# Scores of a chunked linear attention: the second sequence of a pair held with its halves exchanged

## The chip, the cores and the metric

The kernel runs on one NeuronCore of one Trainium2 chip. TensorE multiplies matrices (its records are split into weight loads, PEld, and matmuls, PE), VectorE (DVE) and ScalarE (ACT) do elementwise work and empty PSUM, GpSimd (POOL) issues indirect transfers, and SyncE (SP) issues most others. The metric is the device time of one execution in microseconds.

## The reference

Two blocks follow each other. The first is a gated linear attention: for each of 4 sequences and 8 heads, a 48 by 48 state decays by a gate per key dimension and takes in one outer product per token.

```python
f = 1.0 / (1.0 + np.exp(-f_logit))
for t in range(S):                                   # S = 768, D = 48
    state = f[:, :, t, :, None] * state + np.einsum('bhd,bhe->bhde', k[:, :, t], v[:, :, t])
    y[:, :, t] = np.einsum('bhd,bhde->bhe', q[:, :, t], state)
```

The heads of a token are then joined to a row of 384, and the 3072 rows go through a mixture of experts with two levels of gates: a softmax over 4 groups picks a group, a softmax over the 4 experts of that group picks an expert, and the row's output is the product of both weights times `relu(x @ w1[g, e]) @ w2[g, e]`, with a hidden size of 1024.

## The kernel before

**The attention stage.** A sequence is cut in 6 chunks of 128 tokens. A unit is one chunk of a pair of sequences, so there are 12 units, `i = 0` to `11`; even ones belong to the first pair (`s = 0`), odd ones to the second. Inside a chunk, the recurrence is written as matrix products. With the running sum `cs` of the negative log gates (a matmul with the triangle `tri`, L600), queries are scaled by `exp(-cs)` (`eq`) and keys by `exp(cs)` (`kh`). Then the stages of a unit are:

- `load`, L568 to L575: f, q, k and v arrive on SP's queue with tokens on the partitions, one transfer for each tensor of a unit (two for the first f).
- `c` bounded, `g` gated (exp, ln, `cs`, exp; the last row of `eq` goes to `ends` by a small transfer on POOL's queue), `m` multiplied (VectorE scales q and k).
- `t` turned: 16 transposes put the head dimension on the partitions, two heads to a tile (48 rows at 0 and at 64); ACT copies them to `Tq` and `Tk`.
- `b` decayed, for every second unit: `ends` is turned, and the chunk's decay goes to `decays`.
- `s` scored, L648 to L664: for each of the two sequences, 16 products of 64 keys with all 128 queries fill two PSUM banks (one for each head of a tile); then VectorE multiplies each bank with `tri`, which gives zero where the key is later than the query, and writes `am`.
- `n` stated: products `kh` by `v` give the chunk's own state (`ds`), and VectorE adds and decays it.
- `w` weighed: products of the old state with the queries (L699, not in the first chunk), then of `v` with `am` (L704), into the same banks; ACT copies them to `xT`.
- `d` done: `xT` times the turned gate weights `gw` gives the routing logits, transposed (`lT`); ACT copies them, and a matmul with `fold` turns them and adds the two heads' halves (`lg`, L724); VectorE copies them out.
- `x` listed: 8 transposes bring the rows back to tokens on partitions (`x_ps`), and they are stored.

A product in 32-bit floats leaves two matmul records in the trace, a transpose one: 32 score products are the x64 of a unit.

**Order.** On TensorE, VectorE, ScalarE and SP the order is written out by hand. Lists of steps (`BEGIN` for units 0 to 2, then `EVEN`, `ODD` and a few lists for the last units) call one stage's next part at a time; `s s s s` stands for scores and masks of one sequence, then of the other. `p` writes constants and pads, `h` turns the gate weights (`turn_gates`, L109), and `r` takes the routing of a finished chunk on by one part. In the steady part TensorE's order is x_ps, tr (turns), cs of the next unit, ap (scores), y of L699, lT of the unit before, y of L704, ds, lg. All tiles in PSUM are of one bank and come from one pool of eight. [...]

**The rest.** After unit 11 two early experts, chosen from the first four chunks, run while the routing of the last chunk is finished (until about 168 us); then the 16 experts run one after the other over gathered rows until the end. At the end of the program stands a branch that is not taken with these inputs: `scan` computes the attention in another way when the gates decay too fast.

```python
        EVEN = "l+2 d-2 n-1 r r r x-1 x-1 t t t t g+1 g+1 x-1 r s s s s c+2 w d-1 g+2 w g+2 n m+1 m+1".split()
        ODD = "l+2 d-2 b n-1 r r x-1 x-1 t t t t g+1 g+1 x-1 r s s s s c+2 w d-1 g+2 w g+2 n m+1 m+1 r n".split()
```

## Time and profile before

| | |
|---|---|
| median of 3 runs | 429.12 us (428.27 to 431.68) |
| the profiled execution | 421.97 us, its span 420.2 us |
| PE busy | 408.4 us, 97% of the span |
| DVE busy | 267.1 us, 64% |
| ACT busy | 156.7 us, 37% |
| scores (L660), PE | 768 records, 23.8 us |
| masks (L663), DVE | 48 operations, 29.8 us, mean 682 ns |
| products with v (L704), PE | 384 records, 23.4 us |

The profile is of one execution. A group line gives the source line, the engine, the operation, what is written and read (out<-in), the shape and the count, then busy time and mean duration. In a timeline each line begins with start and length in microseconds from the start of the span; instructions of one kind that follow each other are merged. The chain of work that ended last is followed back from the end to what released each step. A line of waits reads: engine and instruction, then what it waited for, the total in us, how often, and the longest.

### The profile page before, as it was taken

What the parts mean: (1) busy time and instruction counts of PE and PEld (TensorE: products, weight loads), DVE (VectorE), ACT (ScalarE), POOL (GpSimd) and SP (SyncE); (2) the same over time, 40 slices, a digit from 0 to 9 for tenths busy, and PEclk for the clock granted to TensorE, in tenths of its full rate; (3) what the DMA queues carried; (4) which work ended last, traced back from release to release, by engine and by line L of the source; (5) the groups of instructions that cost most, each with busy time, mean ns of one, the idle gap of its engine ahead of it and who ended that gap; (6) DMA issues with size and microseconds to landing.
All of it is one profiled execution on the core that took longest, in us unless ns stands there. A gap on an engine that the chain in (4) does not pass through costs nothing.

```text
span 420.2 us, 10089 instructions
## 1 busy us (share of the span) xinstructions
PE 408.4 (97%) x4067; PEld 383.3 (91%) x4067; DVE 267.1 (64%) x778; ACT 156.7 (37%) x341; POOL 83.2 (20%) x127
## 2 busy tenths in 40 slices
PE   4999999999999999999999999999999999999995
PEld 2888999999889887979999999999999999999992
DVE  6665686868798760650599785495685685595240
ACT  5667666666774421211122121221231231231220
POOL 4000010101012027201021331312222221110230
PEclk9999999999999999999999999999999999999999
DMA  9999999998899819978448385595585785585010
GB/s 168 177 179 178 183 179 179 165 154 146 168 331 404 316 29 365 365 286 308 156 176 288 109 327 189 207 321 162 233 302 146 285 289 192 233 318 159 29 46 25
DMA packets 132121, 88.98 MB, mean 212 GB/s; under 512 B 102630, under 2 KB 122700, under 8 KB 132066
## 3 DMA queue, kind: packets, MB, share of 16 engines
q1 hardware_dynamic: 125666, 75.50, 66.2%
q0 software_dynamic: 5792, 11.92, 9.5%
q8 instruction: 34, 0.56, 0.6%
q10 hardware_dynamic: 608, 0.83, 0.6%
q14 instruction: 21, 0.17, 0.1%
HBM read 78.71 MB, written 9.83 MB: 211 GB/s over the span
## 4 chain that ended last, share of the span: by engine, by line
PE 53%; issue 29%; DMA 8%; POOL 6%; ACT 1%; POOLq 1%; DVE 1%; SPq 0%
PE hp L441 12%; PE yo L477 6%; DMA out_dram<-yt,xg 6%; PE ap L660 5%; PE y L704 5%; PE cs L600 4%; PE yo L462 4%; POOL out_dram L452 4%; PE x_ps L744 3%; PE lT L719 3%; PE tr_q L634 3%; POOL xg L395 2%; PE tr_k L634 2%; PE y L699 2%; PE ds L677 2%
## 5 line engine op out<-in xcount | busy, mean ns | idle before, releaser
L441 PE MATMUL hp<-xe,w 128*128 128x128 f32 (+14 forms) x864 | 138.6, 320 | 0.0
L441 PEld LDWEIGHTS hp<-xe,w 128*128 128x128 f32 x864 | 135.8, 190 | 0.8
L477 PE MATMUL yo<-h,w 128*128 128x230 f32 (+13 forms) x672 | 115.8, 333 | 0.0
L424 DVE STREAM_TRANSPOSE yr<-yT 32x192 f32<-32x192 f32 (+1 forms) x208 | 70.5, 339 | 70.4 <-ACT yT L478 67.8
L477 PEld LDWEIGHTS yo<-h,w 128*128 128x128 f32 x672 | 113.7, 190 | 0.2
L417 DVE STREAM_TRANSPOSE xe<-xg 32x192 f32<-32x192 f32 (+1 forms) x208 | 69.7, 335 | 8.6 <-PE hp L441 5.6
L442 ACT ACTIVATE h<-hp 128x256 f32<-128x256 f32 (+14 forms) x72 | 34.4, 478 | 103.6 <-PE hp L441 103.6
L452 POOL DMA_INDIRECT out_dram<-yt,xg x32 | 34.4, 1076 | 150.4 <-ACT yt L449 144.8
L478 ACT COPY yT<-yo 128x230 f32<-128x230 f32 (+13 forms) x42 | 13.5, 326 | 80.5 <-PE yo L477 80.5
L663 DVE TENSOR_TENSOR am<-ap,tri 128x512 f32<-128x512 f32 x48 | 29.8, 682 | 17.8 <-PE ap L660 17.8
L395 POOL DMA_INDIRECT xg<-x_dram,rows_p x30 | 29.6, 987 | 51.5 <-DMA out_dram<-yt,xg 27.4
L600 PE MATMUL cs<-ld_f,tri 128*128 128x384 f32 x48 | 19.4, 529 | 5.6 <-DVE eq L538 5.5
L660 PE MATMUL ap<-Tq,Tk 48*64 48x128 f32 x768 | 23.8, 272 | 0.3 <-ACT Tk L635 0.3
L704 PE MATMUL y<-am,v 128*64 128x128 f32 x384 | 23.4, 273 | 0.0
L660 PEld LDWEIGHTS ap<-Tq,Tk 48*64 48x64 f32 x768 | 20.8, 133 | 2.1 <-issue 1.1
L704 PEld LDWEIGHTS y<-am,v 128*64 128x64 f32 x384 | 21.4, 137 | 0.6 <-DVE am L663 0.5
L462 PE MATMUL yo<-w,h 128*128 128x384 f32 x64 | 21.3, 486 | 0.0
L462 PEld LDWEIGHTS yo<-w,h 128*128 128x128 f32 x64 | 11.9, 190 | 7.4
L600 PEld LDWEIGHTS cs<-ld_f,tri 128*128 128x128 f32 x48 | 8.6, 200 | 9.7 <-issue 6.0
L607 POOL DMA_DIRECT2D ends<-eq x10 | 5.4, 541 | 60.2 <-ACT eq L601 60.2
L449 ACT ACTIVATE yt<-yr,xg 128x384 f32<-128x384 f32 (+13 forms) x26 | 14.4, 604 | 5.4 <-DVE yr L424 5.4
L707 ACT COPY xT<-y 128x512 f32<-128x512 f32 x24 | 12.9, 589 | 9.3 <-PE y L704 9.3
(170 smaller groups left out, 386.0 us busy)
## 6 DMA issues: line engine op xcount, KB each, us to landing
w<-in_moe_w_dram SPq DMA_DIRECT2D x34, 1536.0 KB, 10.3
qh<-in_q_dram SPq DMA_DIRECT2D x12, 384.0 KB, 6.6
ld_k<-in_k_dram SPq DMA_DIRECT2D x12, 384.0 KB, 6.4
v<-in_v_dram SPq DMA_DIRECT2D x12, 384.0 KB, 7.2
ld_f<-in_f_logit_dram SPq DMA_DIRECT2D x11, 384.0 KB, 6.4
x_dram<-x_kept SPq DMA_DIRECT2D x2, 1536.0 KB, 11.6
x_dram<-x POOLq DMA_DIRECT2D x2, 384.0 KB, 7.2
x_dram<-x ACTq DMA_DIRECT2D x2, 384.0 KB, 7.7
```

Of the source, the lines that this page charges most:

```text
L395: nc.gpsimd.indirect_dma_start(out=w["x"][:, j, :], out_offset=None, in_=x_dram[0:1 + top, :], in_offset=bass.IndirectOffsetOnAxis(ap=rows ...
L417: squares(w, lambda n, k_, rk, g, rg: nc.vector.transpose(out=xT[rg, 0:n, k_], in_=x[rk, 0:n, g]))
L424: squares(w, lambda n, k_, rk, g, rg: nc.vector.transpose(out=y[rk, 0:n, g], in_=yT[rg, 0:n, k_]))
L441: nc.tensor.matmul(hp[:, o, :], lhsT=w1[:, ko, (f + o) * P:(f + o + 1) * P], rhs=w["xT"][:, ko, :], start=(ko == 0), stop=(ko == KO - 1))
L442: nc.scalar.activation(h[:, f:f + 2, :], hp, AF.Relu)
L452: sent = nc.gpsimd.indirect_dma_start(out=out, out_offset=bass.IndirectOffsetOnAxis(ap=w["x"][0:m, j, DM + 1:RW].bitcast(U32), axis=0), in ...
L462: nc.tensor.matmul(yp, lhsT=w["h"][:, fo, :], rhs=w2[:, fo, :], start=(fo == 0), stop=(fo == FO - 1))
L477: nc.tensor.matmul(yp, lhsT=w2[:, fo, m * P:(m + 1) * P], rhs=w["h"][:, fo, :], start=(fo == 0), stop=(fo == FO - 1))
L600: nc.tensor.matmul(cs.rearrange("t h d -> t (h d)"), lhsT=tri, rhs=nl[:, b], start=True, stop=True)
L660: nc.tensor.matmul(ap[r][half, a, :], lhsT=w["Tk"][rows, b, a, half], rhs=w["Tq"][rows, b, a, :], start=True, stop=True)
L663: nc.vector.tensor_tensor(am[:, r], ap[r], tri.unsqueeze(1).broadcast_to((P, HP, P)), OP.mult)
L704: nc.tensor.matmul(ys[r][DP * b:DP * b + DP, a, :], lhsT=w["v"][:, b, 2 * a + r, :], rhs=w["am"][b][:, r, a, :], start=(c == 0 and a == 0) ...
```

## The change

In the second sequence of each pair, the partitions 0 to 63 now hold the later 64 tokens of a chunk, and 64 to 127 the earlier ones. It is loaded that way, so every load of a unit becomes three transfers: the first sequence, and the two halves of the second. The running sum of the second sequence uses an exchanged triangle `tri_s`, its chunk end stands on partition 63 in place of 127, and token numbers are corrected by 64 in either half.

In the scores, the later 64 keys of a chunk are multiplied only with the later 64 queries; the part that would be multiplied by zero is left unwritten in PSUM, and the `am` tiles, now kept through the stage, hold zeros there from the start. With the exchange, the wide products of the two sequences stand in different halves of the array's columns. For units 1 to 11 the products of both sequences alternate in one run of instructions; in unit 0 the first sequence comes first. Masking is done for each bank in two operations of 256 elements each: the later queries of all keys, then the square of the earlier queries with the earlier keys.

Further, the turn of the gate weights on TensorE goes to the start (`h` twice in `BEGIN`), the logits are turned by a transpose and added by a sum on VectorE in place of the matmul with `fold`, and the decays (`b`) and state updates (`n-1`) of odd units go behind the turns. The states of a pair stand in the other order (`1 - b`). The branch that isn't taken follows the new order of tokens.

```diff
+    tri_s = const([P, P], FP32, "tri_s")
...
+    nc.gpsimd.memset(tri_s[0:HF, HF:P], 0.0)
+    nc.gpsimd.memset(tri_s[HF:P, 0:HF], 1.0)
+    for half in (slice(0, HF), slice(HF, P)):
+        nc.gpsimd.tensor_copy(tri_s[half, half], tri[half, half])
...
+        ams = [[kept([P, 2, HP, P], f"am{b}_{i}") for i in range(2)] for b in range(2)]
...
+                if n < 2:
+                    for b in range(2):
+                        nc.vector.memset(ams[b][n][(1 - b) * HF:(2 - b) * HF, :, :, b * HF:(b + 1) * HF], 0.0)
...
-                for b in parts(i) if nm == "f" else (slice(0, 2),):
-                    nc.sync.dma_start(out=heads(w[nm][:, b])[:, :, 0:D], in_=SRC[nm][2 * s + b.start:2 * s + b.stop, :, c * P:(c + 1) * P, :].rearrange("b h t d -> t (b h) d"))
+                for b, u, first, n in ((0, 0, 0, P), (1, 0, HF, HF), (1, 1, 0, HF)):
+                    src = SRC[nm][2 * s + b, :, c * P + first:c * P + first + n, :]
+                    nc.sync.dma_start(out=w[nm][u * HF:u * HF + n, b, :, 0:D], in_=src.rearrange("h t d -> t h d"))
...
-                nc.tensor.matmul(cs.rearrange("t h d -> t (h d)"), lhsT=tri, rhs=nl[:, b], start=True, stop=True)
+                nc.tensor.matmul(cs.rearrange("t h d -> t (h d)"), lhsT=tri_s if b else tri, rhs=nl[:, b], start=True, stop=True)
...
-            for b in range(2):
-                am = sb.tile([P, 2, HP, P], FP32, tag="am", bufs=3, name="am")
-                w["am"].append(am)
-                ap = [bank([P, HP, P], f"ap{r}") for r in range(2)]
+            w["am"] = [ams[b][i % 2] for b in range(2)]
+            aps = [[bank([P, HP, P], f"ap{b}{r}") for r in range(2)] for b in range(2)]
+            squares_ = [(b, u) for b in range(2) for u in range(2)] if i == 0 else [(0, 0), (1, 1), (0, 1), (1, 0)]
+            for group in (squares_[0:2], squares_[2:4]) if i == 0 else (squares_,):
                 for a in range(HP):
                     for r in range(2):
                         rows = slice(DP * r, DP * r + D)
-                        for u in range(2):
-                            half = slice(u * P // 2, (u + 1) * P // 2)
-                            nc.tensor.matmul(ap[r][half, a, :], lhsT=w["Tk"][rows, b, a, half], rhs=w["Tq"][rows, b, a, :], start=True, stop=True)
+                        for b, u in group:
+                            half = slice(u * HF, (u + 1) * HF)
+                            cols = slice(0, P) if b == u else half
+                            nc.tensor.matmul(aps[b][r][half, a, cols], lhsT=w["Tk"][rows, b, a, half], rhs=w["Tq"][rows, b, a, cols], start=True, stop=True)
+            yield
+            for b in range(2):
+                late, diag = slice((1 - b) * HF, (2 - b) * HF), slice(b * HF, (b + 1) * HF)
+                for r in range(2):
+                    ap, am = aps[b][r], w["am"][b]
+                    nc.vector.tensor_tensor(am[:, r, :, late], ap[:, :, late], (tri_s if b else tri)[:, late].unsqueeze(1).broadcast_to((P, HP, HF)), OP.mult)
+                    nc.vector.tensor_tensor(am[diag, r, :, diag], ap[diag, :, diag], tri[diag, diag].unsqueeze(1).broadcast_to((HF, HP, HF)), OP.mult)
                 yield
-                for r in range(2):
-                    nc.vector.tensor_tensor(am[:, r], ap[r], tri.unsqueeze(1).broadcast_to((P, HP, P)), OP.mult)
-                yield
+            yield
...
-            lg = bank([P, 2, NL], "lg")
-            nc.tensor.matmul(lg.rearrange("p b l -> p (b l)"), lhsT=lgT, rhs=fold.rearrange("p b l -> p (b l)"), start=True, stop=True)
-            nc.vector.tensor_copy(groups[c][:, 2 * s:2 * s + 2, :], lg)
+            lg = bank([P, 2, 2, 32], "lg")
+            nc.tensor.transpose(out=lg.rearrange("p r b l -> p (r b l)"), in_=lgT, identity=ident)
+            nc.vector.reduce_sum(out=groups[c][:, 2 * s:2 * s + 2, :], in_=lg[:, :, :, 0:NL].rearrange("p r b l -> p b l r"), axis=AX)
...
-        BEGIN = """c0 g0 p g0 g0 m0 m0 m0 m0 l2 t0 t0 t0 t0 c1 g1 g1 s0 s0 s0 s0 g1 g1 p w0 w0 n0 m1 m1 m1 m1 l3 h x0 x0 x0
+        BEGIN = """c0 h g0 p g0 g0 m0 m0 m0 m0 l2 t0 t0 t0 t0 c1 g1 g1 s0 s0 s0 s0 g1 g1 p w0 w0 n0 m1 m1 m1 m1 l3 h x0 x0 x0
...
-        ODD = "l+2 d-2 b n-1 r r x-1 x-1 t t t t g+1 g+1 x-1 r s s s s c+2 w d-1 g+2 w g+2 n m+1 m+1 r n".split()
+        ODD = "l+2 d-2 r r x-1 x-1 t t t t b n-1 g+1 g+1 x-1 r s s s s c+2 w d-1 g+2 w g+2 n m+1 m+1 r n".split()
...
-            NU - 1: "d-2 b r r n-1 x-1 x-1 t t t t r x-1 r s s s s w d-1 w r r".split(),
+            NU - 1: "d-2 r r n-1 x-1 x-1 t t t t r x-1 r s s s s w b d-1 w r r".split(),
```

## The prediction

> **What bounds the kernel now.** First the page's busy shares, then the chain that ended last for the attention stage, then the timelines of one unit, then the waits.
>
> ```profile
> span 420.2 us, 10089 instructions
> PE 408.4 (97%) x4067; PEld 383.3 (91%) x4067; DVE 267.1 (64%) x778; ACT 156.7 (37%) x341; POOL 83.2 (20%) x127
> ```
>
> TensorE is the engine to shorten. The chain (start, length, what), one unit of the steady part:
>
> ```profile
> 68.34 1.91 PE ap L660 x64
> 70.25 0.87 PE y L699 x32
> 71.12 1.02 PE lT L719 x16
> 72.15 1.75 PE y L704 x32
> 73.90 0.92 PE ds L677 x32
> 74.81 0.34 PE lg L724 x2
> 75.16 0.90 PE x_ps L744 x8
> ```
>
> It stays on PE without a break from unit to unit (10.9 or 11.3 us each), and after 145 us PE goes straight on to the experts. So whatever PE gains or loses per unit reaches the end. One unit by timeline (start, length):
>
> ```profile
> 79.14 1.98 PE L660 MATMUL ap<-Tq,Tk 48*64 48x128 f32 x64
> 80.94 1.05 PE L699 MATMUL y<-Tq,st 48*64 48x128 f32 x32
> 81.92 1.09 PE L719 MATMUL lT<-xT,gw 128*64 128x128 f32 x16
> 82.85 1.92 PE L704 MATMUL y<-am,v 128*64 128x128 f32 x32
> 84.59 1.09 PE L677 MATMUL ds<-v,kh 128*64 128x48 f32 x32
> 80.28 2.48 DVE L663 TENSOR_TENSOR am<-ap,tri 128x512 f32<-128x512 f32 x4 [0.60 <-PE ap L660]
> ```
>
> This is the place to look at. The four masking operations run from 80.28 to 82.76; L704, which reads what they write, starts at 82.85. VectorE starts while PE is still at the second sequence's scores (1.14 us after the first score), and the cover is the rest of the scores, L699 and lT. It is nearly used up, though still whole:
>
> ```profile
> PEld y L704 <- DVE am L663: 0.5, 1, 0.5
> DVE am L663 <- PE ap L660: 17.8, 11, 3.4
> ```
>
> PE waited once for the masks in the whole stage (a unit of the first chunk, without L699); VectorE waited 11 times for scores, so it is free when they come.
>
> [...] 64 score matmuls of 272 ns go through in 1.80 us (79.14 to 80.94), four side by side, and L704's, which share all rows and differ in columns alone, go two side by side (32 in 1.75 us). So each quarter of the array works on its own list: 109 ns for one of 128 columns. [...] ds, two side by side, has 48 columns and takes 0.92/16 = 57.5 ns a pair[...]. A score matmul of 64 columns then costs about 58 ns, not less. [...]
>
> **The change part by part**, in profiled time (421.97 us, its span 420.2).
>
> *Scores.* 32 products of two records each stay; half of them take 64 columns, and the exchange of halves spreads wide and narrow ones equally: each quarter of the array has 8 records of 109 ns and 8 of 58 in place of 16 of 109. 8 x 109 + 8 x 58 = 1.34, with the 0.05 us that the start costs now 1.39 us in place of 1.80. Gain 0.41 us a unit. [...]
>
> *Masks.* Four operations of 512 elements become eight of 256. A step from one VectorE operation to the next is 0.60 us at 512 ((2.48 - 0.68)/3), 0.48 at 384 and 0.87 at 768 (L620 to L623): 1.04 ns an element and a fixed 0.07. So 0.60 - 256 x 0.00104 = 0.334 us at 256, and 0.415 the length of one (0.682 at 512, 0.55 at 384). That half of the partitions are idle in four of them saves nothing. Eight take 7 x 0.334 + 0.415 = 2.75 us in place of 2.48. And they start later: all four PSUM banks are written to the end, since the four (sequence, half) products alternate. Now VectorE starts 0.2 us after half the score stream; then 0.2 us after all of it: 1.39 + 0.21 = 1.60 us after the first score in place of 1.14.
>
> *The wait that comes of it.* PE reaches L704 at 1.39 + 0.98 (L699) + 0.93 (lT) = 3.30. Its second product needs the sixth mask (1.60 + 5 x 0.334 + 0.415 = 3.69), its fourth the eighth, 4.36, with 0.06 for the release 4.42. From there seven products of 2 x 109 ns are left on that column half: end at 4.42 + 0.05 + 1.53 = 6.00. Now L704 ends 5.45 after the first score (84.59 - 79.14). So a unit loses 0.55 us between scores and ds, although its scores are 0.41 shorter. Queued behind the waiting product: the rest of L704, ds, lg, then x_ps; ACT's copies of y and the next unit's turns wait with them.
>
> *Logits.* lg, two matmuls against the fold, becomes one transpose. From ds to x_ps's second product 0.15 us less (one of the two steps of 0.13 and 0.11, and the longer start of x_ps). VectorE's copy of 0.198 us becomes a sum of 80 elements (0.23), on no path. Sum per steady unit: +0.55 - 0.15 = **+0.40 us**; units 3 to 10: +3.2.
>
> *The last unit* has no cs between its turns and its scores; now its scores start behind the first sequence's copies, then they wait for Tk of the second (0.4 to 0.8 later). The decay turn moved into its cover gives 0.35 back, two lg give 0.3: together +0.2.
>
> *The first units.* Unit 0: masks ready some 0.15 later; two more memsets of 0.48 ahead of the first clamp (0.82 idle there) cost 0.15; the next two fit beside the 0.72 us that VectorE waits for eq. The gate turns (gw_ps, 1.02 us of chain at 18.13) go ahead of cs at 5.47, where PE is idle; issued on ACT's queue by 1.7 us, the gate loads are small: -1.0. Without that cover the same 1.0 us delays cs. Unit 1: cs and ds lie between scores and L704, so no mask wait, but the scores start after the second Tk copy (0.6 later): +-0. Unit 2: the same, and VectorE, with its constants behind later masks, gives its operands late: half of the lead is lost. The moved decay turn ends the one wait for an ends transfer (0.38 us); POOL sends four rows in place of two, same issue. State updates that go behind the turns on VectorE have 2.7 us of idle time there; the decay copy follows the Tk copies on ACT, ahead of eq, which nobody waits for within 0.2 us. The late table work (`mine`) takes an xT buffer when the units are done: nothing. Sum: about -0.9.
>
> *Loads.* Same 192-byte rows, but 12 transfers a unit on SP's queue in place of 4.
>
> ```profile
> 74.13 0.37 SPq L575 DMA_DIRECT2D ld_k<-in_k_dram  x1
> 74.59 1.22 SPq L575 DMA_DIRECT2D qh<-in_q_dram  x1
> 75.91 1.53 SPq L575 DMA_DIRECT2D ld_f<-in_f_logit_dram  x1
> 77.50 3.52 SPq L575 DMA_DIRECT2D v<-in_v_dram  x1
> ```
>
> An issue costs 0.37 us unhindered, otherwise what the engines need, about 2 us a tensor: 12 x 0.37 = 4.4 us in 10.9. A unit's loads are used some 10 us later, so in the steady part they hide. At the start they don't: the second f slice now comes in two, +0.2 us, and k of unit 1 is waited for (1.0 us). Bounds 0 to 1.5 us; I take 0.2.
>
> Sum: -0.9 + 3.2 + 0.2 + 0.2 = +2.7 us, 424.7 profiled. The median of the runs shown is 429.12, 7.1 us above the profiled one; the difference is added there: **431.8 us**, 0.6% more. 1% (4.3 us) is about what a measurement of this kernel can tell.
>
> **Rivals.**
> - *The mask wait doesn't arise* (other side). Mechanism: the masks for the first sequence come early enough, or L704 can run its free column half ahead, so that L704 follows lT. Place: L704's first four products; price: -0.55 in place of +0.40 a unit, 0.56 x 9 and the lead of the start, -6.2 us: 422.9. It decides when the eighth mask ends before 3.5 us. Against it: eight operations can't take less than 2.67 us on these rows, and nothing of them can start before the banks are full. Chance 0.15.
> - *Scores don't shrink*: narrow and wide products wait for each other, 1.80 us as now. Then masks start at 2.01, L704 ends at 6.41: +0.96 - 0.15 = +0.8 a unit, with the lost lead of units 1 and 2 +7: 436. For it: the trace shows only equal widths side by side. Against: pairs and fours already leave program order. 0.23.
> - *Loads slow the start*: some 35 transfers, most on half the partitions, where 12 were in the first 20 us, when the queue is never idle; k of units 0 and 1 later by 1 to 2 us on top of the forecast: 434. 0.12.
> - The forecast, 0.50, with its own range 429.5 to 434.
>
> **Numbers.** Faster by over 1% (below 424.8): the first rival, 0.15. Slower by over 1% (above 433.4): nearly all of the second rival (0.22), half of the third (0.06) and a fifth of the forecast (0.10), 0.38. Between: 0.47. The range leaves out most of the first rival and the top of the second: 425 to 437.
>
> **What would show it.** L660 at 1.4 us a unit; eight operations at the masks, 2.75 us from first to last; in the waits PE behind the masks about 0.9 us in each of 9 units where there was one of 0.5; lT to L704 with a hole on PE; gw_ps before cs; no wait of gt for ends. Wrong would make it: no wait there; L660 at 1.8 us; a VectorE step at 256 elements far from 0.33 us; a first cs later than 5.9 us.

## The result and the profile after

The changed kernel takes **440.0 us** (median; 439.9 to 440.6), the kernel before 428.7 beside it: ratio **1.025**, 95% interval 1.020 to 1.030. The forecast was 431.8 us, so the sign was that of the sum (+2.7 us) and the size was not: +11.3 us. A second comparison on another chip gave 434.1 against 422.9, the same +11.3. Two executions, one of ds_ahead (442.6 us) and one of all_back (535.0 us), were in a slower state and are left out of the totals below.

The profiled execution of the kernel before (421.97 us) lacked a stall of TensorE of some 5.4 us, early in the main experts. It goes with the chip, not with the kernel: the first profile after and the ten profiles from chips on which the kernel before takes 429 to 430 us have it, the eight from chips on which it takes 423 us do not. So below, totals are compared with the kernel before run on the same chip, and profiles stage by stage.

The page of the kernel after, its span and the busy time of the engines: TensorE's share falls from 97 to 94%.

```profile
span 438.1 us, 10326 instructions
PE 413.1 (94%) x4055; PEld 381.4 (87%) x4055; DVE 277.0 (63%) x830; ACT 157.2 (36%) x341; POOL 85.0 (19%) x131
```

Unit 7 in the timeline after (start, length; in brackets the idle time before and its releaser), to be held against unit 6 in the prediction:

```profile
95.79 1.56 PE L676 MATMUL ap<-Tq,Tk 48*64 48x128 f32 x62
...
97.18 0.28 PE L720 MATMUL y<-Tq,st 48*64 48x128 f32 x2
...
97.19 0.23 PE L676 MATMUL ap<-Tq,Tk 48*64 48x64 f32 x2
...
97.38 0.42 DVE L682 TENSOR_TENSOR am<-ap,tri 128x256 f32<-128x256 f32 x1 [2.02 <-PE ap L676]
97.72 0.41 DVE L683 TENSOR_TENSOR am<-ap,tri 64x256 f32<-64x256 f32 x1
98.05 0.41 DVE L682 TENSOR_TENSOR am<-ap,tri 128x256 f32<-128x256 f32 x1
...
98.38 0.41 DVE L683 TENSOR_TENSOR am<-ap,tri 64x256 f32<-64x256 f32 x1
98.72 0.41 DVE L682 TENSOR_TENSOR am<-ap,tri_s 128x256 f32<-128x256 f32 x1
...
99.14 0.43 DVE L683 TENSOR_TENSOR am<-ap,tri 64x256 f32<-64x256 f32 x1
99.14 0.92 PE L725 MATMUL y<-am,v 128*64 128x128 f32 x6
...
99.59 0.42 DVE L682 TENSOR_TENSOR am<-ap,tri_s 128x256 f32<-128x256 f32 x1
...
100.03 0.43 DVE L683 TENSOR_TENSOR am<-ap,tri 64x256 f32<-64x256 f32 x1
...
100.49 0.56 DVE L595 TENSOR_SCALAR ld_f<-ld_f 128x768 f32<-128x768 f32 x1
100.51 1.39 PEld L725 LDWEIGHTS y<-am,v 128*64 128x64 f32 x25 [0.70 <-DVE am L683]
...
101.98 0.27 PE L725 MATMUL y<-am,v 128*64 128x128 f32 x1
```

The scores did shrink: their records run over 1.62 us (95.79 to 97.41) in place of 1.98, and the products with the old state (L720) start 1.39 us after the first score in place of 1.80. The masks start 1.59 us after the first score (1.60 was predicted). But they end at 100.46, 3.08 us later, and TensorE, which reached the products with v at 99.14, stands for the last one. Those products end 6.47 us after the first score, before the change 5.62. A steady unit takes 11.60 or 12.14 us in place of 10.87 or 11.33.

The chain of waits after, in total us, times, longest:

```profile
DVE am L682 <- PE ap L676: 18.9, 11, 3.7
PEld y L725 <- DVE am L683: 9.7, 17, 1.1
DVE st L705 <- ACT decays L660: 5.2, 4, 1.8
PE y L725 <- DVE am L683: 4.9, 10, 0.9
```

The wait of TensorE for the masks was one of 0.5 us; now it is there in nine of the twelve units (0 and 3 to 10), about 1.0 us of weight loads in a steady one. Two more things are new. From 95 to 150 us, SP waits:

```profile
SPq L589 <- DMA ends<-eq: 10.3, 1, 10.3
SPq L390 <- DMA ends<-eq: 6.8, 1, 6.8
```

SP loads inputs and weights and has no business with `ends`. For 10.3 us it stood ahead of k of unit 11, and all behind it came late:

```profile
122.29 1.70 SPq L589 DMA_DIRECT2D ld_k<-in_k_dram  x3
...
133.10 0.39 SPq L390 DMA_DIRECT2D w<-in_moe_w_dram  x1
```

The stores of the kept rows stand behind it too (the first goes at 128.8 us in place of 111.1). The second of them lands at 144.7, only then are the first early expert's rows gathered (145.6), and TensorE stands for them:

```profile
153.17 0.52 PE L438 MATMUL xg_ps<-ident,xg 128*128 128x128 f32 x3 [3.23 <-DMA xg<-x_dram,rows_e]
```

The first weights were issued at 119.06 before. And at the start, the first score comes at 13.44 us in place of 11.65.

### The profile page after: what moved, and what is told of

Read it like the earlier page. It is cut to its first block, busy times and chain, and to the rows that moved or that the text cites. A ratio compares the mean times of both kernels' runs of the same rounds, so it can differ in the third digit from the quotient of the medians.

```text
span 438.1 us, 10326 instructions
## 1 busy us (share of the span) xinstructions
PE 413.1 (94%) x4055; PEld 381.4 (87%) x4055; DVE 277.0 (63%) x830; ACT 157.2 (36%) x341; POOL 85.0 (19%) x131
## 4 chain that ended last, share of the span: by engine, by line
PE 34%; issue 30%; DMA 10%; DVE 10%; POOL 5%; ACT 3%; another core or an unknown queue 2%; SPq 2%; POOLq 1%; DVEq 1%; ACTq 0%
PE hp L448 10%; PE yo L484 6%; DMA out_dram<-yt,xg 6%; POOL out_dram L459 3%; PE y L725 3%; PE ap L676 3%; PE yo L469 2%; PE cs L614 2%; DVE am L682 2%; POOL xg L402 2%; SPq L589 2%; DVE am L683 2%; DMA xg<-x_dram,rows_e 2%; PE x_ps L765 1%
## 5 line engine op out<-in xcount | busy, mean ns | idle before, releaser
L725 PE MATMUL y<-am,v 128*64 128x128 f32 x384 | 28.8, 277 | 5.6 <-DVE am L683 4.9
L725 PEld LDWEIGHTS y<-am,v 128*64 128x64 f32 x384 | 22.9, 137 | 10.2 <-DVE am L683 9.7
L676 PE MATMUL ap<-Tq,Tk 48*64 48x128 f32 (+1 forms) x768 | 21.7, 254 | 0.9 <-ACT Tk L650 0.8
L676 PEld LDWEIGHTS ap<-Tq,Tk 48*64 48x64 f32 x768 | 19.2, 136 | 3.5 <-ACT Tk L650 2.2
L682 DVE TENSOR_TENSOR am<-ap,tri 128x256 f32<-128x256 f32 x24 | 9.9, 415 | 18.9 <-PE ap L676 18.9
L683 DVE TENSOR_TENSOR am<-ap,tri 64x256 f32<-64x256 f32 x48 | 20.0, 417 | 0.3
L649 PE MATMUL tr_q<-ident,qh 128*128 128x128 f32 x96 | 15.2, 285 | 1.1 <-DVE qh L635 1.1
```

The lines of the kernel that those rows point to most:

```text
L676: nc.tensor.matmul(aps[b][r][half, a, cols], lhsT=w["Tk"][rows, b, a, half], rhs=w["Tq"][rows, b, a, cols], start=True, stop=True)
L682: nc.vector.tensor_tensor(am[:, r, :, late], ap[:, :, late], (tri_s if b else tri)[:, late].unsqueeze(1).broadcast_to((P, HP, HF)), OP.mult)
L683: nc.vector.tensor_tensor(am[diag, r, :, diag], ap[diag, :, diag], tri[diag, diag].unsqueeze(1).broadcast_to((HF, HP, HF)), OP.mult)
L725: nc.tensor.matmul(ys[r][DP * b:DP * b + DP, a, :], lhsT=w["v"][:, b, 2 * a + r, :], rhs=w["am"][b][:, r, a, :], start=(c == 0 and a == 0) ...
```

## The experiments

Totals are given as the difference of medians from the kernel before in the same comparison; the intervals of the ratios reach 0.15 to 0.7% to either side, so most totals are good to about 2 us, the best to 0.6 and the worst to 3. A period in a trace mostly repeats within 0.02 us between two executions of a kernel.

### before_three_loads: the transfers alone

The kernel before, with its loads cut like the changed kernel's, but not exchanged.

```diff
-                for b in parts(i) if nm == "f" else (slice(0, 2),):
-                    nc.sync.dma_start(out=heads(w[nm][:, b])..., in_=SRC[nm][...])
+                for b, u, n in ((0, 0, P), (1, 0, P // 2), (1, 1, P // 2)):
+                    at = u * P // 2
+                    nc.sync.dma_start(out=w[nm][at:at + n, b, :, 0:D], in_=SRC[nm][2 * s + b, :, c * P + at:c * P + at + n, :]...)
```

> The kernel before, with nothing changed but its loads: each tensor of a unit in three transfers (first sequence, and two halves of the second, not exchanged). If the number of transfers is a cost of its own, the first score comes at about 13 us in place of 11.65, the period of a steady unit stays at 10.87 and 11.33 us, the weights of the early experts are issued later than 119.1 us, and the total grows by 2 to 6 us. If the loads hide, as the prediction had it (+0.2 us), the first score stays below 12.0 us and the total within 1 us.

Measured +6.0 us (ratio 1.0125, 1.007 to 1.018). First score at 12.54 us (11.65 and, in before_again, 11.15 in the kernel before), steady periods unchanged, first weights at 127.2, and unit 11 follows unit 10 after 12.98 us in place of 9.12. So the transfers cost much, none of it in the steady part: +0.9 at the start, the rest at the end of the stage.

### ends_pool: is it the counter?

In the trace after, each of SP's transfers names one of eight counters, semaphores 101 to 108, mostly in turn. Those of q of unit 10 take 103, 104 and 106; 105 is left out, and is that of ACT's `ends` transfer of unit 10, which is issued later, at 120.29 us. SP comes round to 105 with k of unit 11, and waits 10.3 us, until 122.2, when `ends` has landed. In the trace before, with 4 transfers a unit, the turn met `ends` elsewhere: it has 107, between the stores of the kept rows (106 and 109).

```diff
+        def side_ends(i):
+            return nc.gpsimd
...
-                    side(i).dma_start(out=ends[c][4 * s:4 * s + 4, :], ...)
+                    side_ends(i).dma_start(out=ends[c][4 * s:4 * s + 4, :], ...)
```

> The changed kernel, with the small transfer of ends for units 10 and 11 on POOL's queue in place of ACT's. The trace of the changed kernel has SP waiting 10.3 us for that transfer before it loads k of unit 11 (issued at 122.3 us). Theory: this wait comes from a completion counter that the two queues share, and it holds back the weights: k of unit 11 is then issued at about 114.5 us, the first weights at about 125 in place of 133.1, and the total falls by 3 to 8 us. Rival: SP is late because it has three times as many transfers to issue; then the weights stay at 132 to 134 us and the total within 1 us.

Measured +8.4 us, 2.9 less than the changed kernel. k of unit 11 went at 112.09, the first weights at 124.22. SP's longest waits for inputs and weights in the same stretch are now ordinary ones (with three lines more in the program, L592 is L589 above):

```profile
SPq L390 <- DMA x_dram<-x_kept: 7.6, 2, 5.0
SPq L592 <- DVE kh L641: 2.5, 1, 2.5
```

The wait for the shared counter is shown (10.3 us, and none for `ends` with the transfer moved). What it is worth is less sure than the totals look: their intervals overlap (1.015 to 1.026 against 1.020 to 1.030), and the profile of ends_pool is 2.3 us ahead by unit 1 already, for a reason at the start of the program (see after_again). By the traces, the stretch from the first score of unit 11 to the first product of the early experts tells: 13.85 and 12.29 us in the two profiles of the changed kernel, 11.24 in ends_pool and 10.73 in odd_back_ends. That is 1.6 us between after_again and odd_back_ends, which ran on the same chip, and 2.6 between the first two; 3 to 8 were expected.

### orders_back and odd_back_ends: the moved decays and state updates

The list for NU - 3 is changed likewise; in orders_back that for NU - 1 too; odd_back_ends has the `ends` transfers on POOL's queue.

```diff
-        ODD = "l+2 d-2 r r x-1 x-1 t t t t b n-1 g+1 g+1 ..."
+        ODD = "l+2 d-2 b n-1 r r x-1 x-1 t t t t g+1 g+1 ..."
```

> The changed kernel with decays and state updates of odd units back in the places of the kernel before (three lists). Theory: in unit 9 the state update behind the turns waited for ACT's copy of the decays and pushed the routing and the masks; with the old lists masks of unit 9 start 1.6 us after the first score in place of 2.38, the step from unit 9 to unit 10 falls from 12.90 to about 12.1 us, the gather for the early experts is issued 2 to 5 us earlier than 145.6, and the total falls by 2 to 5 us. Rival: the place of these steps costs nothing; the total stays within 1 us, and a wait of gt for ends comes back.

> The changed kernel with all ends transfers on POOL's queue and decays and state updates of odd units back in their old places (the last unit's stay as changed). Theory: without the counter's wait the moved steps show: the step from unit 9 to unit 10 falls from 12.90 to 12.1 us and the total is 0.5 to 2 us below that of the kernel with only the ends moved (8.4 us above the kernel before). Rival: the place of these steps costs nothing; the total stays 8 to 9 us above the kernel before.

In both, unit 9's masks start 1.6 us after the first score again, not 2.38, and the step from unit 9 to 10 falls to 12.15 and 12.14 us: that mechanism holds and is worth 0.75 us. In the totals it doesn't show: orders_back +11.5 us (the counter still held SP until 120.7, and unit 11 again turned its decays at the start of its list, 11.0 us after unit 10 in place of 9.9), odd_back_ends +8.0 against +8.4 with only `ends` moved. Expected were 2 to 5 us less for orders_back and 0.5 to 2 for odd_back_ends.

### ds_ahead: other work ahead of the wait

The other lists are changed in the same way.

```diff
-        EVEN = "... s s s s c+2 w d-1 g+2 w g+2 n m+1 m+1"
+        EVEN = "... s s s s c+2 w d-1 n g+2 w g+2 m+1 m+1"
```

> The changed kernel with the products of the unit's own state (ds, 0.92 us of TensorE) ahead of the products of v with am, in units 2 to 10. Theory: the steady unit is longer because TensorE stands at am; with 0.92 us more of work before it that wait falls from about 0.9 to 0.1 to 0.4 us, a unit takes 11.0 and 11.5 us in place of 11.60 and 12.14, and the total falls by 4 to 5 us. Rival: something else sets the unit (turns, copies, loads), and the wait only moves behind am's products: periods and total within 1 us of the changed kernel's.

Measured +9.2 us (1.012 to 1.025, not told apart from the changed kernel); periods 11.48 and 11.70, so only 0.12 and 0.44 less. The products with v now start at 4.27 us and still end at 6.47. ds had been cover for ACT: x_ps, now next in line, waits for ACT's copy of y (0.4 us in most units), and VectorE's products with q and k still start behind the masks. A wait moved as the rival said, but not all of the gain went with it.

### full_scores: old scores and masks, all else changed

Each sequence is scored and then masked in two operations of 512 elements, in place of eight of 256 after both.

```diff
-                            cols = slice(0, P) if b == u else half
-                            nc.tensor.matmul(aps[b][r][half, a, cols], ..., rhs=w["Tq"][rows, b, a, cols], ...)
+                            nc.tensor.matmul(ap[r][half, a, :], ..., rhs=w["Tq"][rows, b, a, :], ...)
...
+                for r in range(2):
+                    nc.vector.tensor_tensor(w["am"][b][:, r], ap[r], (tri_s if b else tri)..., OP.mult)
```

> The changed kernel with the scores and masks of the kernel before (all 128 queries for all keys, one sequence after the other, four masks of 512 elements), all else as changed: exchanged halves, three transfers, lists, logits, gate weights. Theory: the narrow scores with their eight masks are what lengthens a steady unit; with the old ones the periods of units 3 to 8 are 10.87 - 0.15 = 10.7 and about 11.2 us in place of 11.60 and 12.14, and the total falls by 5 to 8 us from 440, to 432 to 435: what is left above the kernel before is the loads, the queue and the moved state updates. Rival: loads and lists lengthen the units; then periods stay above 11.3 and 11.8.

Measured +4.0 us (1.0102, 1.006 to 1.014), periods 10.76 and 11.30 us. So scores and masks are what lengthens a steady unit, by 0.84 us, and nothing else does: with the loads, lists and queues left as changed, the periods are those of before_parts (10.76 and 11.25).

### masks_order: why are the masks 3.08 us long?

Seven steps of 0.334 us and one length of 0.415 would be 2.75. In the timeline above, the first sequence's follow each other by 0.33 us, and so does the second's first operation; the steps after it are 0.42 to 0.46, one length: no overlap. In the second sequence the square begins on partition 64, the other operation on 0.

```diff
                 for r in range(2):
                     nc.vector.tensor_tensor(am[:, r, :, late], ...)
+                for r in range(2):
+                    ap, am = aps[b][r], w["am"][b]
                     nc.vector.tensor_tensor(am[diag, r, :, diag], ...)
```

> The changed kernel with the masks of a sequence in another order: the two operations on the later queries, then the two on the squares. In the second sequence the steps are 0.42, 0.44, 0.44 us where the first has 0.34, 0.33, 0.33. Theory: VectorE doesn't overlap two operations whose first partitions differ (0 and 64); then the steps of the second sequence become 0.33, 0.42, 0.33, the eight masks take 2.9 us in place of 3.08, and a steady unit is 0.15 to 0.2 us shorter (total -1 to -2 us). Rival: an operation that begins on partition 64 is slow in itself, or the waits of the second sequence do it: then the third and last steps stay at 0.42 to 0.44 and the masks at 3.0 to 3.1 us.

Timeline (pairs of equal operations are merged):

```profile
94.00 0.76 DVE L682 TENSOR_TENSOR am<-ap,tri 128x256 f32<-128x256 f32 x2 [2.02 <-PE ap L676]
94.67 0.74 DVE L685 TENSOR_TENSOR am<-ap,tri 64x256 f32<-64x256 f32 x2
95.33 0.74 DVE L682 TENSOR_TENSOR am<-ap,tri_s 128x256 f32<-128x256 f32 x2
96.08 0.77 DVE L685 TENSOR_TENSOR am<-ap,tri 64x256 f32<-64x256 f32 x2
```

The pairs' starts are 0.67, 0.66 and 0.75 us apart: one step of 0.42 is left, at the change from partition 0 to 64, and two equal squares on partition 64 follow each other by 0.35, so the place alone is not what is slow. The masks take 2.85 us, a unit 11.38 and 11.92 us, 0.22 less. The trace agrees with the theory. The total, +6.7, fell by more than the 2 us that nine such units give; this profile is 2.5 us ahead of the changed kernel's by unit 1, for the reason under after_again.

### by_sequence: start the masks early, let the scores be long

```diff
-            squares_ = [...] if i == 0 else [(0, 0), (1, 1), (0, 1), (1, 0)]
-            for group in (squares_[0:2], squares_[2:4]) if i == 0 else (squares_,):
+            squares_ = [(b, u) for b in range(2) for u in range(2)]
+            for group in (squares_[0:2], squares_[2:4]):
```

> The changed kernel with the scores of all units grouped by sequence, as unit 0 has them (products narrow and wide as changed). Theory: a quarter of the array that has narrow products waits for its wide neighbours in the same group, so the scores take 1.80 us again, but the masks begin after the first sequence, 1.14 us after the first score in place of 1.59, and end 0.45 us earlier; the unit is set by the masks, so its period falls by 0.4 us, to 11.2 and 11.7 us, though its scores take longer: total -3 to -4 us. Rival: the length of the scores counts; then the period stays or grows by up to 0.4 us.

Measured +6.8 us, periods 11.15 and 11.69.

```profile
91.86 0.42 DVE L682 TENSOR_TENSOR am<-ap,tri 128x256 f32<-128x256 f32 x1 [1.57 <-PE ap L676]
...
94.26 2.37 PE L725 MATMUL y<-am,v 128*64 128x128 f32 x31
...
94.51 0.43 DVE L683 TENSOR_TENSOR am<-ap,tri 64x256 f32<-64x256 f32 x1
```

The first score is at 90.72. The records of the scores run over 1.81 us, so about half of the gain on TensorE is gone (1.98 before, 1.62 in the changed kernel), and it reaches the products with v at 3.54 us (before 3.71, changed 3.35). Yet the unit is 0.45 us shorter, because the masks start at 1.14. The masks, not the scores, set the unit. As for the order within the array: the last of the scores in the timeline, at 92.14, 92.15 and 92.25 us, are wide, where in the changed kernel the last two are narrow (97.19). There each half of the columns gets a wide and a narrow product in turn; that none has to run ahead of the others then is the author's reading of the difference, not shown.

### before_parts: the small parts

The kernel before with the gate weights turned at the start and the logits turned by a transpose.

```diff
-        BEGIN = """c0 g0 p g0 ...
+        BEGIN = """c0 h g0 p g0 ...
-            nc.tensor.matmul(lg..., lhsT=lgT, rhs=fold..., start=True, stop=True)
-            nc.vector.tensor_copy(groups[c][:, 2 * s:2 * s + 2, :], lg)
+            nc.tensor.transpose(out=lg..., in_=lgT, identity=ident)
+            nc.vector.reduce_sum(out=groups[c][:, 2 * s:2 * s + 2, :], in_=lg[:, :, :, 0:NL]..., axis=AX)
```

> The kernel before with two parts of the change alone: gate weights turned at the start, and logits turned by a transpose with the sum on VectorE in place of the matmul with fold. Theory, from the prediction: -0.15 us for each of 8 steady units, -1.0 us in the first, -0.3 in the last: the first score of unit 1 comes 0.8 to 1.0 us earlier, the periods are 10.7 and 11.2 us, and the attention stage ends 2 to 2.5 us earlier; the total falls by 1 to 3 us from that of the kernel before. Rival: these parts hide, or the sum on VectorE takes its time from something else: attention ends within 0.5 us of the kernel before.

**426.2 us, 3.6 less than the kernel before** (0.992, 0.989 to 0.994): faster than both. From unit 0 to unit 1 it takes 9.52 us in place of 10.54, and steady units 10.76 and 11.25 in place of 10.87 and 11.33.

### before_again and after_again

> The kernel before once more, for a second profile. Its profiled execution took 421.97 us, 6.8 us less than its median. If the profiled one was an exception, this one takes 427 to 431 us, with the same periods of 10.87 and 11.33 us in the attention stage, and the difference lies in one place behind it: the first pass of the main experts, which takes 19 to 22 us in the three variants of the changed kernel profiled since, against 15.5 us in the first profile of the kernel before. If the profile is typical of how it runs, the first pass takes 15 to 16 us again.

> The changed kernel once more. In its profile the eight turns of k in unit 0 took 1.9 us; in three of the variants with the same start they took 1.1. If that was one execution's slow array, the first score comes at about 11.9 us here unless it is slow again, and the end of the attention stage is 1.5 us earlier or the same; the total is 10 to 12 us above the kernel before either way. If the start of the changed kernel is slow by itself, the turns take 1.9 us again and the first score comes at 13.4.

before_again took 428.6 us with the same periods but for one unit (11.57 us), and the stall was where expected, in the first pass of the main experts: the records between 168.99 and 175.40 us, which run without a break in the first profile (168.18 to 180.37), have holes there.

```profile
168.99 1.86 PE L441 MATMUL hp<-xe,w 128*128 128x128 f32 x15
...
172.88 0.27 PE L441 MATMUL hp<-xe,w 128*128 128x128 f32 x1 [0.92 <-issue]
...
175.40 11.27 PE L441 MATMUL hp<-xe,w 128*128 128x230 f32 x48 [0.61 <-DVE xe L432]
```

The holes are 2.6 us, and the mean granted clock of TensorE between 140 and 200 us is 0.97, 1.00 in the first profile. The products with the second weights begin 17.5 us after the first record of this pass, in place of 12.0.

after_again lacks that stall and took +11.3 us all the same. Its start was slow again: first score at 13.30 us. The turns of unit 0 in the first profile after, and in ends_pool, which has the same start:

```profile
9.84 1.97 PE L649 MATMUL tr_q<-ident,qh 128*128 128x128 f32 x8 [1.08 <-DVE qh L635]
11.60 1.92 PE L649 MATMUL tr_k<-ident,kh 128*128 128x128 f32 x8
```

```profile
9.55 1.12 PE L652 MATMUL tr_q<-ident,qh 128*128 128x128 f32 x8 [0.81 <-DVE qh L638]
10.51 1.10 PE L652 MATMUL tr_k<-ident,kh 128*128 128x128 f32 x8
```

The same 16 transposes go at half the rate: 0.21 us from one to the next in place of 0.11. So do the products for `cs` ahead of them, in all twenty profiles (records of 0.84 to 1.01 us, in the steady part mostly 0.49). The program thus begins at half rate in all twenty, and what differs is when the full rate comes: in the first profile after not before the first scores, so that those took 2.56 us in place of 1.81 and unit 1's scores start 2.3 us later than in ends_pool. What brings the full rate was not shown. In the ten profiles in which the zeros of `am` stand on VectorE at the start, the turns of q begin at 9.5 to 9.9 us, and those of k are at half rate throughout (1.91 or 1.92 us) five times. In the ten others the turns of q begin at 8.1 to 9.0 us, soon after cs, and the full rate comes before the turns of k are over (1.04 to 1.48 us). All five with half rate throughout have late turns, but in five others the turns are as late, and the pause ahead of them doesn't tell the two apart: it is 0.6 to 1.1 us in the first five and 0.5 to 0.9 in the others. The totals of the variants contain this start too, fast or slow, and only one execution of each has a trace.

### memsets_pool: the zeros off VectorE

```diff
-                        nc.vector.memset(ams[b][n][...], 0.0)
+                        nc.gpsimd.memset(ams[b][n][...], 0.0)
```

> The changed kernel with the zeros of the am tiles written by POOL in place of VectorE. Theory: two of these operations (1.11 us) stand ahead of VectorE's first product with q and hold it from 7.9 to 9.3 us; with them gone the turns of q begin at 8.4 to 8.8 us in place of 9.6 to 9.9, TensorE stands idle for less time ahead of them, and the first score comes at 11.0 to 11.8 us (13.44 in the changed kernel's profile, 11.9 where its turns ran at full rate); the total is 0.5 to 1.5 us lower. Rival: the second loads of f and the exponentials set the first score; then it stays within 0.2 us of 11.9 or 13.4, and the total within 0.5 us.

Measured +8.4 us. The turns of q begin at 8.39 us as expected, but the first score comes at 12.00, not 11.0 to 11.8: the second half of f, clamped at 5.35, and the exponentials behind it set it, as the rival had it, and ends_pool, with the zeros on VectorE, comes as early (11.86). The eight turns of q still go at half rate, those of k (1.12 us) and the scores at full rate, so unit 1's scores start 2.2 us earlier than in the first profile after. The total fell by 2.9 us, but the intervals overlap (1.016 to 1.026 against 1.021 to 1.031), and three profiles with the zeros on VectorE have the full rate as early.

### three_loads_ends and all_back: a wait in place of a wait

three_loads_ends is before_three_loads with the edit of ends_pool. all_back is full_scores with that edit, no zeros written, and the three lists as before.

> The kernel before with three transfers for each tensor, and with all ends transfers on POOL's queue. Theory: most of the 6.0 us that three transfers cost in the kernel before come from the completion counters that SP's and ACT's queues share, not from the transfers; then k of unit 11 is issued at about 109 us in place of 116.4, unit 11 follows unit 10 after 9 to 10 us in place of 12.98, the first weights go at about 120 in place of 127.2, and the total falls from 434.75 to 430 to 432 us. Rival: the transfers themselves fill SP's queue; then the total stays at 433 to 436 us.

> The changed kernel with scores and masks, the three lists and VectorE's memsets as before, and all ends transfers on POOL's queue. What is left of the change: the exchanged halves with three transfers, the early turn of the gate weights and the logits by a transpose. Theory: with the masks, the shared counter and the moved steps gone, the cost that remains is the loads' at the start (0.9 us) and the gain is that of the two small parts (3.6 us): 426 to 429 us. Rival: the exchange or three transfers cost more than that in other places; then 430 to 434 us.

Measured +5.8 and +3.3 us: as differences (the kernel before takes 423.2 us on this chip), the rivals' side in both. SP no longer stood at the counter (k of unit 11 at 110.9 and 106.6 us), but unit 11 followed unit 10 after 15.99 and 14.17 us. three_loads_ends in the timeline:

```profile
125.88 0.54 POOL L611 DMA_DIRECT2D ends<-eq  x1
135.37 0.49 PEld L648 LDWEIGHTS gt<-ident,ends 4*128 4x128 f32 x4 [3.52 <-issue]
```

The 4 KB of `ends` took 9.4 us to land, while the kept rows were stored and the first weights came (1.5 MB each); in the unit before, on the same queue, 3.4. `gt` stands on TensorE ahead of all of unit 11 there, and after that pause TensorE was slow: the first transpose of x_ps behind it took 0.47 us (0.27 at 103.27 us in the trace after). The mean granted clock of the whole execution is 0.990, and 0.995 in all_back, where the two other profiles on this chip have 0.997 and 0.999. In the changed kernel `gt` of unit 11 comes late, so it had been safe from that.

### three_loads_late_b and all_back_late_b

```diff
-            NU - 1: "d-2 b r r n-1 x-1 x-1 t t t t r x-1 r s s s s w d-1 w r r".split(),
+            NU - 1: "d-2 r r n-1 x-1 x-1 t t t t r x-1 r s s s s w b d-1 w r r".split(),
```

> The kernel before with three transfers for each tensor, all ends transfers on POOL's queue, and the last unit's decays turned late, as in the changed kernel. three_loads_ends took the shared counter away, but unit 11 then waited for ends on POOL's queue (16.0 us from unit 10 to 11). Theory: with neither wait, unit 11 follows after 9 to 10 us, and the total is 0.5 to 2 us above the kernel before: three transfers cost little more than the start's 0.5 to 0.9 us. Rival: the transfers themselves cost 4 to 6 us in other places; then the total stays 4 us or more above it.

> The changed kernel with scores, masks, memsets and the lists of odd units as before and all ends transfers on POOL's queue, but the last unit's decays late, as changed. all_back had 14.2 us from unit 10 to unit 11, of which TensorE waited some 4 for ends. Theory: that step falls to 9 to 10 us and the total to 0 to 3 us below the kernel before, so that scores with masks, the shared counter and the moved steps are all of the loss. Rival: the total stays 2 us or more above the kernel before.

all_back_late_b: 423.2 against 422.9, **+0.3 us** (1.001, 0.9995 to 1.002), between what was expected and the rival; unit 11 after 9.71 us. three_loads_late_b: **+5.1 us** (1.009, 1.006 to 1.013), on the rival's side: three transfers cost 2.5 to 5.4 us by the interval even without the counter. Its trace shows 0.75 us more from unit 0 to 1, and in units 10 and 11 two holes on TensorE, of 1.9 and 0.9 us, the longer in the middle of the products with v, where the instruction waits for nothing that is recorded:

```profile
PE y L708 <- issue: 1.9, 1, 1.9
PE y L703 <- issue: 0.9, 1, 0.9
```

What held TensorE there was not shown. three_loads_ends has such a hole too, of 0.9 us, in the products with v of unit 10 (131.18 us).

### narrow_best and before_parts_late_b

narrow_best is the changed kernel with the edits of by_sequence, masks_order and odd_back_ends together; before_parts_late_b is before_parts with the late `b` in the last unit.

> The changed kernel with its narrow scores kept, but grouped by sequence, the masks of a sequence in the order late, late, square, square, all ends transfers on POOL's queue, and decays and state updates of odd units in their old places. If the measured effects add up, a steady unit takes 11.15 - 0.22 = 10.9 and 11.4 us, still 0.15 above that with the old scores and masks (10.76 and 11.25), and the total is 8.0 - 4.5 - 1.5 = 2 us above the kernel before (1 to 4). If they overlap, the total stays 4 us or more above; if the narrow scores are a gain once the masks start early, the periods fall below 10.76 and 11.25 and the total below the kernel before.

> The kernel before with the gate weights turned at the start, the logits by a transpose, and the last unit's decays turned late. The first two alone made 3.6 us (0.8%) less. Theory: the third takes 0.3 us off TensorE ahead of the last unit's scores, so the total is 3.5 to 4.5 us below the kernel before. Rival: the late turn ends in the way of the last logits: 2 to 3.5 us below.

narrow_best: 430.8 against 429.3, +1.5 us (1.002 to 1.006), periods 10.93 and 11.42: the effects add up, and even so the narrow scores leave a unit 0.17 us longer than the old ones (10.76, 11.25). before_parts_late_b: **425.9 against 429.3, -3.5 us** (0.992, 0.990 to 0.994), not told apart from before_parts.

## Why the prediction was wrong

The runs make a ladder from the kernel before to the kernel after, one part at a time (differences of totals, good to about 1 us in the first two rows, 2 in the third and 3 in the last two):

| step | from, to | us | predicted |
|---|---|---|---|
| gate weights early, logits by transpose, last decays late | before, before_parts_late_b | -3.5 | -2.8 |
| exchanged halves in three transfers, `ends` on POOL's queue | to all_back_late_b | +3.8 | +0.2 |
| narrow scores, eight masks, zeros at the start | to odd_back_ends | +7.7 | +5.7 |
| decays and updates of odd units moved | to ends_pool | +0.4 | -0.4 |
| SP behind ACT's `ends` | to after | +2.9 | none |

The predicted column groups the prediction's own terms: 8 x -0.15, -1.0, and -0.65 in the last unit; then 8 x 0.55, 0.85 for the last unit's wait on Tk, 0.3 of masks and zeros in unit 0 and 0.2 in unit 2; and -0.4 for the end of the wait for `ends`. They add up to 2.7, the measured ones to 11.3. For the last two rows the traces are sharper than the totals: 0.75 us in the step from unit 9 to 10, and 1.6 to 2.6 us behind the counter.

*Scores*: right. Narrow and wide ones mix, and what follows them starts after 1.39 us, as predicted. by_sequence shows that it takes their alternation.

*Masks*: the start right to 0.01 us, the wait in the right place and of the right sign, the length mis-sized: 3.08 us in place of 2.75. The failed step is "a step from one VectorE operation to the next ... 0.334 us at 256", which took the overlap of operations on the same partitions for all eight; three steps and the one out of the masks were 0.42 to 0.46. (That the idle half of the partitions saves nothing held: the squares, on 64, took 0.41 to 0.43 us, the others, on 128, 0.41 to 0.42.) With it, the masks ended 0.3 us later than forecast, and a unit lost 0.84 us to scores and masks in place of 0.55; masks_order gave 0.22 of it back. (The prediction's end of the products with v, 5.45 us, is the start of ds; their last record ends at 5.62. The difference is not touched by this.)

*Logits*: right in sign, 0.11 and 0.08 us in place of 0.15. *Gate weights early*: right (1.02 us). *Zeros at the start*: "the next two fit beside the 0.72 us that VectorE waits for eq" failed. The pair took 1.11 us and pushed the first product with q from 7.65 to 9.29 us; alone it would have cost little, as memsets_pool shows, but half of the profiles with these zeros have the half rate into the first scores, which costs some 2 us by unit 1.

*State updates and decays*: "have 2.7 us of idle time there" failed. VectorE waited up to 1.8 us for ACT's copy of the decays, 5.2 in all; in unit 9 that pushed the routing and the masks by 0.8 us. In the totals it doesn't show.

*Loads*: the worst step, put at 0.2 us and measured at 3.8, and at 2.9 more (1.6 to 2.6 by the traces) for the counter, which the sum did not have. "An issue costs 0.37 us unhindered" took the shortest of the trace as the price; after, the median of 144 issues is 0.63 us, so a tensor keeps SP for 2 us as before, and the queue of loads, which ended a unit's issues early, is busy without a break until about 99 us (71 before). "in the steady part they hide" was right for the units' periods, but the queue also feeds the stores of the kept rows and the weights of the experts, and it ran late into the end of the stage. The profiles of before_parts_late_b and all_back_late_b place the 3.8 us: 1.0 ahead of the first score, 1.1 between units 2 and 3 (where two executions of the kernel before differ by 0.6 already), 0.7 between units 10 and 11, and 1.0 from there to the early experts. What holds TensorE in each of these places stays open. And the prediction didn't ask whose counter a transfer on SP's queue waits for.

*The base*: of the 7 us between the profiled execution and the median, 5.4 lay in a stall outside the stage; so adding the difference as a constant was sound.

The first rival (no mask wait) and the second (scores don't shrink) are refuted by the steady unit; the third (loads slow the start, 434) had the right suspect in the wrong place.

## What to carry to other kernels

Work that is shortened ahead of a queue must be followed to the engine that consumes it: 0.4 us less on TensorE was worth nothing, since VectorE got its input later and in more, smaller operations. Count transfers by the issue time that the busy queue shows, not by its shortest, and look in the trace at what a transfer waits for besides its data: a counter that two queues take in turn tied k of unit 11, and the weights behind it, to a small transfer of another engine for 10.3 us here. Parts of a change are to be measured one by one; here two small ones were a gain of 3.6 us that the rest hid.

## What was not expected of the hardware

- VectorE's masks (256 elements) follow each other by 0.33 to 0.35 us, but by 0.42 to 0.46 where the partitions start elsewhere than the last one's: after, and masks_order, where one such step is left among a unit's masks and takes 0.42.
- A small transfer was slow beside large ones: in three_loads_ends, `ends`, 4 KB, took 9.4 us to land while rows and weights of 1.5 MB each were under way, and 3.4 us in the unit before.
- A pause of TensorE went with slow work behind it: in before_again, holes of 2.6 us came with a mean granted clock of 0.97 over 60 us, and the pass was longer by 5.5 us; in three_loads_ends, after a pause of 3.5 us, a transpose took 0.47 us in place of 0.27.
- A unit's scores, half of them narrow, run over 1.62 us where wide and narrow ones alternate (after) and over 1.81 where they are grouped by sequence (by_sequence); all wide ones take 1.98 (before).
- The same 16 transposes at the same place of the program took 2.1 us in ends_pool and 3.7 in the first profile after: TensorE came to its full rate at different times.
